# Other PSUM homes, another PE order in the double steps, later rank products and earlier row loads in an SSD and mixture-of-experts kernel

## The chip, the cores and the metric

One NeuronCore of a Trainium2 chip. The metric is the device time of one execution in microseconds (us). A profile of one execution stands beside it. PE is the matrix engine, DVE the vector engine, ACT the scalar engine, POOL is GpSimd, and SP issues the plain transfers. PEld is PE's loading of the standing operand, which runs beside PE's products.

## What is computed

A Mamba2 state-space block over 4 batches, 8 heads, 768 steps, head size 32 and state size 16, and behind it a layer of 8 experts in which each of the 3072 tokens goes to the one expert with the highest logit:

```python
for c in range(nc):                                   # chunks
    cum = np.cumsum(la, axis=-1)
    M = np.einsum('bhin,bhjn->bhij', Cc, Bc) * L      # L: decay between steps, causal
    y_intra = np.einsum('bhij,bhjd->bhid', M, xc)
    y_inter = np.einsum('bhin,bhnd->bhid', Cc, state) * decay_to_i[:, :, :, None]
    y[:, :, sl] = y_intra + y_inter
    state = decay_full[:, :, None, None] * state + np.sum(Bx, axis=2)
...
logits = x @ w_gate                                   # x: (3072, 256), the block's y
expert_idx = np.argmax(logits, axis=1)
for e in range(E):                                    # 8 experts
    h = np.maximum(xe @ w1[e], 0.0)                   # 256 -> 1024
    out[mask] = gate_w[mask, None] * (h @ w2[e])      # 1024 -> 256
```

## The kernel before

The first part works in chunks of 128 steps: 6 chunks x 4 batches make 24 units, two of them make a double step, and a loop runs over 12 double steps d = 0 to 11 (and once more for what is left). Unit n = 2d + s. The work of a double step, with the names that the rows use:

- ACT makes cm (C masked for two heads' halves, `masked_C`), POOL makes xp (x over the running decay, `scaled_x`).
- PE multiplies B and cm into g (`scores`, four PSUM banks), DVE multiplies g with the causal mask into M (`weigh`), PE multiplies M and xp into y (`y_own`) on top of the part from the carried state (`y_old`, lhsT S). y has two banks.
- PE forms the new state in A_ps: B times xp (`own`, eight products of 32x64) and the carried S by an identity product. ACT scales A_ps into S (`state`). A_ps lies in columns 320 to 448 of bank 0 of r.
- ACT copies y to SBUF (`turned`, tile yT). One double step later PE turns it (`rows`, tile r, two banks) so that tokens lie on partitions, which also gives the eight gate logits, and DVE scales r into the token rows and the logits (`rows_out`).

Token rows come in five groups of 6, 6, 4, 2 and 6 units. When a group is complete, `choose` (DVE, one exponential on ACT) finds each token's expert, `rank` (PE) multiplies triangular and all-ones matrices with the choice to count each token's place, DVE picks the place (rb, pos), `gates` and `count` finish, and `place` sends the 128 rows of a unit to x_hbm by an indirect transfer from POOL, two units per double step. After the fourth group `cut` fills up the first 256 rows per expert with zero rows (`lack`), and after the fifth `over` fills the rest.

The second part has 16 jobs: 8 experts with 256 rows each, then 8 with 192 rows each. A job's rows are loaded from x_hbm by SP (`m_load`), transposed in pairs of 128x128 on PE into xT_ps (one bank of its own) and copied by DVE (`m_xT`, `xT_of`), multiplied with w1 into h_ps (three buffers) and through ACT's ReLU into hT (`m_h`), and multiplied with w2 into y_ps one job later (`m_y`, `m_half`), scaled by ACT and sent to the output by POOL. In the middle of a job's h, `between` loads job i+2's rows, transposes job i+1's, and issues the weights of expert i+2. Weights of experts 0 and 1 are loaded inside the first part's loop.

The order is written by hand: each engine does its instructions in the order of the program, and a wait on one holds all behind it. PE, ACT and DVE do not work in one PSUM bank at the same time: where two touch the same bank, the later in the program waits for the earlier. A transfer from x_hbm waits for all earlier placements into it, and a placement for all earlier loads from it. SP issues transfers in order and stops at one whose wait is open.

Of the kernel before, what the change touches and what calls it, by code (L numbers as in the profile page):

```python
# [20 lines left out]
CH = 128  # L21
# [6 lines left out]
CUT = 4  # L28
# [15 lines left out]
def ssd_then_moe(ctx, tc, xs_in, ae_in, wgx, w_gate, w1, w2, gx, gb, gc, ga, out):  # L44
# [63 lines left out]
    A_ps = r_ps[:, 0, 320:448]  # L108

    def early_consts():  # L110
        make_identity(nc, ident)
# [211 lines left out]
    def rank(g):  # L323
# [13 lines left out]
        nc.tensor.matmul(p, lhsT=Tmat, rhs=oh, start=False, stop=True, skip_group_check=True)  # L337
        rb = sm2.tile([128, RG, E], FP32, name="rb")[:, 0:n]
# [63 lines left out]
    def m_load(i):  # L402
        p, e = jobs[i]
        if p == 0:
            xs = mo.tile([128, 2, W], FP32, name="xs", bufs=4)
# [3 lines left out]
        xs = mo.tile([128, 2, W], FP32, name="xs", bufs=4)  # L409
# [9 lines left out]
    def xT_of(xs, pp):  # L419
        p = xT_ps[:, turns[0] % 2]  # L420
# [18 lines left out]
    def up(xT, w, f, n, pp):  # L439
        p = pp.tile([128, 512], FP32, name="h_ps", tag="h", bufs=3)  # L440
# [45 lines left out]
    def general(gp, pp):  # L486
# [4 lines left out]
        with tc.For_i(0, NB) as b, tc.For_i(0, NH) as h:  # L491
# [7 lines left out]
            yp = [pp.tile([128, 512], FP32, name="h_ps", tag="h", bufs=3) for _ in range(2)]  # L499
# [63 lines left out]
    with tc.manual_schedule():  # L563
        load_ae()
# [15 lines left out]
        exs = {}  # L580
        for d in range(ND + 1):
            k = d - 1
            if d < ND:
                y_old(d)
                own(d)
                weigh(2 * d)
                weigh(2 * d + 1)
                if d == 0:
                    decays(1)
                    totals()  # L590
                if d == 1:
                    weakest()
                if d + 1 < ND:
                    for s in range(2):
                        masked_C(2 * d + 2 + s)
                        scaled_x(2 * d + 2 + s, nc.gpsimd)
                y_own(d, 0)
                if d + 1 < ND:
                    scores(2 * d + 2)
            if 0 <= k < ND - 1:  # L600
                rows(k)
            if d < ND:
                y_own(d, 1)
                state(d)
                turned(d)
                if d + 1 < ND:
                    scores(2 * d + 3)
            if 0 <= k < ND - 1:
                rows_out(k)
                u = 2 * k + 1  # L610
                if u == R0[grp[u]] + RGS[grp[u]] - 1:
                    exs[d] = grp[u]
            if d == 0:
                route_consts()
# [3 lines left out]
            if 2 <= d < 10:  # L618
                i = 2 * (d - 2)
                for j in (i, i + 1):  # L620
                    load_w(*divmod(j // 4, 2), j % 4)
            if d in exs:
                q = exs[d]
                e_ = choose(q)
                rank(q)
                gates(q, e_)
                count(q)
                todo += list(range(R0[q], R0[q] + RGS[q]))
                if q == CUT - 1:
                    for n in todo:  # L630
                        place(n)
                    todo = []
                    cut()
                    for i in range(2):
                        m_load(i)
            for _ in range(2):
                if todo:
                    place(todo.pop(0))
        att.close()
# [94 lines left out]
```

## Time and profile before

| what | value |
|---|---|
| median of 3 runs | 354.86 us (354.09 to 356.09) |
| profiled execution | 352.56 us, span 350.8 us |
| PE busy | 289.5 us, 83% of the span |
| DVE, ACT, POOL busy | 70.0, 90.6, 85.6 us |
| mean granted PE clock | 0.918 of full |
| moved by DMA | 36.69 MB, 105 GB/s |

The span runs from the first to the last instruction. The first part fills some 113 us of it, the 16 jobs the rest. PE's busy share is a mean over both parts. A row of the timeline gives the start in us, the time in us, the engine, the line, the operation with its tiles (out<-in), how many instructions are merged, and in brackets the idle time of the engine before it and what ended that.

### The profile page before, as it was taken

The page shows a single profiled execution, that of the slowest core. Times are in us where ns is not written, and L with a number is a line of the kernel's source. Part 1 is how long each engine was busy: PE and PEld are TensorE (multiplying, and loading weights), DVE is VectorE, ACT ScalarE, POOL GpSimd, SP SyncE. Part 2 cuts the span into 40 slices and gives each one's busy share as a digit, 9 for nine tenths or more (in the row PEclk, how much of TensorE's full clock was granted, in tenths as well). Part 3 has the DMA queues.
Part 4 walks back from the last instruction along what each step waited for, and adds up shares of the span by engine and source line. Part 5 has one row for each costly group of instructions (what it writes and reads, how often), then busy time and mean ns, then how long its engine had stood idle before and what let it go on. Part 6 is the DMA issues. An engine that isn't in the chain of part 4 may idle for free.

```text
span 350.8 us, 5397 instructions
## 1 busy us (share of the span) xinstructions
PE 289.5 (83%) x2131; PEld 233.5 (67%) x2131; DVE 70.0 (20%) x168; ACT 90.6 (26%) x265; POOL 85.6 (24%) x171
## 2 busy tenths in 40 slices
PE   2388698596666792599999999999999999999990
PEld 1245465364434571488888888888989889788870
DVE  1736544636335500000000000001000010010000
ACT  2234322323301221013223132232322233223310
POOL 1521182353281187011202112021121111201121
PEclk9999869878668967599999999999999999999998
DMA  7434357450022032795482735100100101100000
GB/s 248 156 132 150 128 201 237 130 187 17 15 103 80 0 107 103 215 341 157 158 252 91 245 104 195 46 32 13 62 30 22 43 23 39 46 2 13 13 34 12
DMA packets 19906, 36.69 MB, mean 105 GB/s; under 512 B 2940, under 2 KB 6751, under 8 KB 19872
## 3 DMA queue, kind: packets, MB, share of 16 engines
q1 hardware_dynamic: 16896, 28.61, 25.4%
q0 software_dynamic: 2976, 7.64, 5.8%
q8 instruction: 19, 0.31, 0.4%
q14 instruction: 15, 0.12, 0.1%
HBM read 28.60 MB, written 8.16 MB: 105 GB/s over the span
## 4 chain that ended last, share of the span: by engine, by line
PE 63%; DVE 12%; issue 10%; POOL 6%; ACT 3%; DMA 2%; another core or an unknown queue 2%; POOLq 0%; SPq 0%; ACTq 0%; DVEq 0%
PE h_ps L443 23%; PE y_ps L473 21%; PE r L280 5%; DVE M L223 4%; PE g L218 4%; PE y L265 4%; POOL x_hbm L349 4%; PE xT_ps L423 3%; PE y_ps L482 2%; ACT S L246 2%; POOL out_dram L457 2%; DVE rows L289 1%; DVE xT L433 1%; DMA xs_n<-in_xs_dram 1%
## 5 line engine op out<-in xcount | busy, mean ns | idle before, releaser
L443 PE MATMUL h_ps<-xT,w 128*128 128x256 f32 (+1 forms) x512 | 106.9, 364 | 0.0
L443 PEld LDWEIGHTS h_ps<-xT,w 128*128 128x128 f32 x512 | 93.1, 197 | 9.0 <-issue 1.2
L473 PE MATMUL y_ps<-w,hT 128*128 128x256 f32 x384 | 85.3, 379 | 0.0
L473 PEld LDWEIGHTS y_ps<-w,hT 128*128 128x128 f32 x384 | 72.7, 190 | 9.5
L452 ACT ACTIVATE hT<-h_ps 128x256 f32<-128x256 f32 (+1 forms) x128 | 45.6, 357 | 84.1 <-PE h_ps L443 76.3
L457 POOL DMA_INDIRECT out_dram<-yo,xs x24 | 23.6, 984 | 167.0 <-ACT yo L463 154.7
L433 DVE COPY xT<-xT_ps 128x256 f32<-128x256 f32 x24 | 10.2, 424 | 182.9 <-PE xT_ps L423 182.9
L463 ACT ACTIVATE yo<-y_ps,xs 128x256 f32<-128x256 f32 x24 | 11.4, 474 | 74.2 <-PE y_ps L473 70.8
L223 DVE TENSOR_TENSOR M<-g,mask 128x1024 f32<-128x1024 f32 x24 | 28.2, 1216 | 4.7 <-PE g L218 4.0
L218 PE MATMUL g<-cm,xs_n 32*128 32x256 f32 x192 | 21.2, 516 | 9.1 <-ACT cm L206 6.2
L349 POOL DMA_INDIRECT x_hbm<-rows,pos x24 | 23.9, 995 | 5.2 <-issue 4.1
L265 PE MATMUL y<-M,xp 128*32 128x128 f32 x384 | 20.3, 338 | 5.4 <-DVE M L223 3.3
L423 PE MATMUL xT_ps<-ident,xs 128*128 128x128 f32 x48 | 10.5, 303 | 15.3 <-DMA xs<-x_hbm 10.6
L280 PE MATMUL r<-turn,yT 128*128 128x160 f32 x96 | 21.3, 379 | 0.0
L280 PEld LDWEIGHTS r<-turn,yT 128*128 128x128 f32 x96 | 17.8, 243 | 5.0 <-issue 5.0
L218 PEld LDWEIGHTS g<-cm,xs_n 32*128 32x128 f32 x192 | 10.0, 229 | 15.8 <-issue 9.0
L211 POOL TENSOR_TENSOR xp<-xs_n,Ei 128x256 f32<-128x256 f32 x22 | 13.7, 636 | 22.9 <-PE y L265 13.3
L246 ACT ACTIVATE S<-r,et 128x32 f32<-128x32 f32 x40 | 8.2, 288 | 42.9 <-PE r L280 35.6
L265 PEld LDWEIGHTS y<-M,xp 128*32 128x32 f32 x384 | 11.5, 130 | 11.4 <-issue 5.8
L423 PEld LDWEIGHTS xT_ps<-ident,xs 128*128 128x128 f32 x48 | 6.1, 148 | 18.7 <-DMA xs<-x_hbm 11.0
L289 DVE TENSOR_TENSOR rows<-r,Er 128x512 f32<-128x512 f32 x12 | 8.3, 692 | 41.2 <-ACT S L246 22.4
L206 ACT ACTIVATE cm<-xs_n,par 128x128 f32<-128x128 f32 x48 | 15.3, 398 | 0.0
(110 smaller groups left out, 128.8 us busy)
## 6 DMA issues: line engine op xcount, KB each, us to landing
w<-in_w_dram SPq DMA_DIRECT2D x64, 256.0 KB
xs_n<-in_xs_dram SPq DMA_DIRECT2D x24, 320.0 KB
xs<-x_hbm SPq DMA_DIRECT2D x8, 258.0 KB
xs<-x_hbm SPq DMA_DIRECT2D x8, 129.0 KB
xh<-x_hbm SPq DMA_DIRECT2D x8, 64.5 KB
x_hbm<-rows,pos POOLq DMA_INDIRECT x24
out_dram<-yo,xs POOLq DMA_INDIRECT x24
turn<-in_wgx_dram SPq DMA_DIRECT2D x1, 160.0 KB
```

Of the source, the lines that this page charges most:

```text
L206: nc.scalar.mul(t[:, u], st[n]["CT"], par[:, u:u + 1])
L218: nc.tensor.matmul(g_ps[:, q, n % 2], lhsT=st[n]["BT"][r], rhs=st[n]["cm"][r].rearrange("p u i -> p (u i)"), start=True, stop=True)
L223: nc.vector.tensor_tensor(out=t, in0=g_ps[:, :, n % 2].rearrange("p q (u i) -> p q u i", u=2), in1=bc(mask[:, None, None, :], [128, 4, 2, ...
L246: nc.scalar.mul(new[:, s, u * D:u * D + D], A_ps[:, 64 * s + u * D:64 * s + u * D + D], et[:, 2 * d + s, u:u + 1])
L265: nc.tensor.matmul(y_ps[o:o + D, h // 4, CH * s:CH * s + CH], lhsT=st[n]["xp"][:, D * h:D * h + D], rhs=st[n]["M"][:, h], start=first, sto ...
L280: nc.tensor.matmul(r_ps[:, s, 160 * t:160 * t + 160], lhsT=sd[d]["yT"][:, t, CH * s:CH * s + CH], rhs=turn[:, t].rearrange("p h e -> p (h ...
L349: s_ = nc.gpsimd.indirect_dma_start(out=x_hbm[:, :], out_offset=bass.IndirectOffsetOnAxis(ap=at, axis=0), in_=row, in_offset=None)
L423: nc.tensor.transpose(p[:, t], xs[:, 128 * t:128 * t + 128], ident)
L443: nc.tensor.matmul(p[:, 0:n], lhsT=w[:, c:c + 128], rhs=xT[:, t, 0:n], start=(t == 0), stop=(t == KT - 1))
L452: nc.scalar.activation(ex[i]["hT"][:, f, 0:n], q, func=ACT.Relu)
L457: return nc.gpsimd.indirect_dma_start(out=out[:, :], out_offset=bass.IndirectOffsetOnAxis(ap=tok, axis=0), in_=yo[:, :], in_offset=None, b ...
L473: nc.tensor.matmul(p, lhsT=ex[i]["hT"][:, f, 128 * t:128 * t + 128], rhs=w_sb[e][1][:, f * DM:f * DM + DM], start=(f == 0), stop=(f == FT ...
```

## The change

Six things change:

- A_ps moves from bank 0 of r to columns 256 to 384 of bank 0 of y. The transposes of the experts' rows move from a bank of their own to the two banks of r, one pair in each in turn; the freed bank is a fourth buffer for h. M has four buffers for three.
- The order inside a double step is another: rows of the step before come first, then own, y_old, both halves of y_own, turned, state, and then both scores of the next step. The loads of the step come at its head, rows_out behind the scores.
- rank, and with it the placing, is done one double step after choose, behind that step's y_own; three placements are issued per double step for two. Group 5's choose and count stand ahead of job 0, its rank in the middle of job 0.
- Of the weights only those of expert 0 are loaded in the loop (double steps 5 to 10); those of expert 1 are issued when the first three jobs' rows have been.
- m_load runs three jobs ahead (three jobs after cut, job 3 at the head of the middle of job 0, then i+3); xs has five buffers for four.
- At the start decays(0) stands ahead of masked_C, one of the first two xp goes to POOL, and a one-element ACT operation stands ahead of all.

```diff
@@
-    A_ps = r_ps[:, 0, 320:448]
+    A_ps = y_ps[:, 0, 256:384]
     def early_consts():
+        nc.scalar.mul(spare, spare, 1.0)
...
-        t = wk.tile([128, 4, 2, CH], FP32, name="M", bufs=3)
+        t = wk.tile([128, 4, 2, CH], FP32, name="M", bufs=4)
...
         nc.tensor.matmul(p, lhsT=Tmat, rhs=oh, start=False, stop=True, skip_group_check=True)
+
+    def ranked(g):
...
         rb = sm2.tile([128, RG, E], FP32, name="rb")[:, 0:n]
...
-            xs = mo.tile([128, 2, W], FP32, name="xs", bufs=4)
+            xs = mo.tile([128, 2, W], FP32, name="xs", bufs=5)
...
     def xT_of(xs, pp):
-        p = xT_ps[:, turns[0] % 2]
+        p = r_ps[:, turns[0] % 2, 0:256].rearrange("p (t m) -> p t m", t=KT)
...
-        p = pp.tile([128, 512], FP32, name="h_ps", tag="h", bufs=3)
+        p = pp.tile([128, 512], FP32, name="h_ps", tag="h", bufs=4)
...
+        nc.vector.memset(spare, 0.0)
         load_ae()
...
         par_consts()
+        decays(0)
         for n in range(2):
             masked_C(n)
             scores(n)
-        decays(0)
         for n in range(2):
-            scaled_x(n, nc.vector)
+            scaled_x(n, (nc.vector, nc.gpsimd)[n])
...
-        for d in range(ND + 1):
+        wq = [5, 6, 7, 8, 9, 9, 10, 10]
+        for d in range(ND):
             k = d - 1
-            if d < ND:
-                y_old(d)
-                own(d)
-                weigh(2 * d)
-                weigh(2 * d + 1)
...
-                y_own(d, 0)
-                if d + 1 < ND:
-                    scores(2 * d + 2)
-            if 0 <= k < ND - 1:
-                rows(k)
-            if d < ND:
-                y_own(d, 1)
-                state(d)
-                turned(d)
-                if d + 1 < ND:
-                    scores(2 * d + 3)
-            if 0 <= k < ND - 1:
-                rows_out(k)
...
+            for j, at in enumerate(wq):
+                if at == d:
+                    load_w(0, *divmod(j, 4))
...
+            if k >= 0:
+                rows(k)
+            own(d)
+            y_old(d)
+            weigh(2 * d)
+            weigh(2 * d + 1)
+            for s in range(2):
+                y_own(d, s)
+            turned(d)
...
+            state(d)
+            q = late.get(d)
+            if q is not None:
+                rank(q)
+                ranked(q)
+                todo += list(range(R0[q], R0[q] + RGS[q]))
+            if d + 1 < ND:
+                for s in range(2):
+                    scores(2 * d + 2 + s)
+            if k >= 0:
+                rows_out(k)
...
                 e_ = choose(q)
-                rank(q)
+                count(q)
                 gates(q, e_)
...
+                late[d + 1] = q
-            for _ in range(2):
+            for _ in range(3):
                 if todo:
                     place(todo.pop(0))
+            if d == ND - 2:
...
+                cut()
+                for i in range(3):
+                    m_load(i)
...
-        xT_ps = pp.tile([128, 2, KT, 128], FP32, name="xT_ps")
         m_xT(0, pp)
         rows(ND - 1)
         rows_out(ND - 1)
+        e_ = choose(CUT)
+        count(CUT)
+        for k in range(8):
+            load_w(1, *divmod(k, 4))
...
                 if i == 0:
+                    m_load(3)
                     q = CUT
-                    e_ = choose(q)
                     rank(q)
+                    ranked(q)
...
-                    if i + 2 < len(jobs):
-                        m_load(i + 2)
+                    if i > 0 and i + 3 < len(jobs):
+                        m_load(i + 3)
                     m_xT(i + 1, pp)
```

PE in a double step of the loop, before. y<-xs_n,S is y_old, r<-xp and r<-S,ident are own with the carried state, y<-M is y_own, r<-turn is rows, g is scores; x4, x8 and x16 count products:

```order
L257 MATMUL y<-xs_n,S 64x128 x8
L232 MATMUL r<-xp,xs_n 32x64 x8
L237 MATMUL r<-S,ident 128x128
L265 MATMUL y<-M,xp 32x128 x8
L218 MATMUL g<-cm,xs_n 128x256 x4
L280 MATMUL r<-turn,yT 128x160 x4
L265 MATMUL y<-M,xp 32x128 x8
L218 MATMUL g<-cm,xs_n 128x256 x4
```

The same engine and step now:

```order
L281 MATMUL r<-turn,yT 128x160 x4
L233 MATMUL y<-xp,xs_n 32x64 x8
L238 MATMUL y<-S,ident 128x128
L258 MATMUL y<-xs_n,S 64x128 x8
L266 MATMUL y<-M,xp 32x128 x16
L219 MATMUL g<-cm,xs_n 128x256 x8
```

The two g stand together at the end, rows at the head, and own and its identity product write into y.

SP from the last weights of the first part to the fourth job's rows, before. xs<-x_hbm are rows of a job, w_1 and w_2 weights of experts 1 and 2:

```order
L164 DMA xs_n<-in_xs_dram 128x640 x2
L176 DMA w_1_88<-in_w_dram 128x512 x4
L406 DMA xs<-x_hbm 128x2x258 x3
L176 DMA w_2_89<-in_w_dram 128x512 x4
L176 DMA w_2_90<-in_w_dram 128x512 x4
L406 DMA xs<-x_hbm 128x2x258
```

Now:

```order
L177 DMA w_0_86<-in_w_dram 128x512 x4
L413 DMA xs<-x_hbm 128x2x258 x3
L177 DMA w_1_87<-in_w_dram 128x512 x4
L177 DMA w_1_88<-in_w_dram 128x512 x4
L413 DMA xs<-x_hbm 128x2x258
L177 DMA w_2_89<-in_w_dram 128x512 x4
L177 DMA w_2_90<-in_w_dram 128x512 x4
L413 DMA xs<-x_hbm 128x2x258
```

In the order before, the third load of the three stands in the program behind group 5's placements; now all of the three and the one behind expert 1's weights stand ahead of them, and the last row here is the first behind them.

DVE behind the rows of a group's last units, before (l to oh_all are choose, rb and pos rank, se and rows<-se gates, cs count, M the next step's):

```order
L299 TENSOR_REDUCE l<-lg_132 128x48
L301 TENSOR_REDUCE mx<-l 128x6
L303 TENSOR_TENSOR sub<-l,mx 128x48
L308 SCALAR_TENSOR_TENSOR eq<-sub,rev_e 128x48
L311 TENSOR_REDUCE m_513<-eq 128x6
L312 TENSOR_TENSOR oh_all<-eq,m_513 128x48
L339 TENSOR_TENSOR rb<-r,oh_all 128x48
L340 TENSOR_REDUCE pos<-rb 128x6
L318 TENSOR_REDUCE se<-ex 128x6
L320 RECIPROCAL rows_127<-se 128x6
L344 TENSOR_REDUCE cs<-oh_all 128x8
L223 TENSOR_TENSOR M<-g,mask 128x1024 x2
```

Now, from the choice's last operation on:

```order
L313 TENSOR_TENSOR oh_all<-eq,m_511 128x48
L351 TENSOR_REDUCE cs<-oh_all 128x8
L319 TENSOR_REDUCE se<-ex 128x6
L321 RECIPROCAL rows_127<-se 128x6
L224 TENSOR_TENSOR M<-g,mask 128x1024 x2
L346 TENSOR_TENSOR rb<-r,oh_all 128x48
L347 TENSOR_REDUCE pos<-rb 128x6
L290 TENSOR_TENSOR rows_128<-r,Er 128x2x256
```

rb and pos, which need PE's rank products, stand behind the next step's M.

## Rows read from the trace of the kernel before

**Rows 1.** The page, part 2: granted PE clock in 40 slices, tenths of full

```profile
PEclk9999869878668967599999999999999999999998
```

**Rows 2.** Busy time by stretch: from:to, length, then busy of each engine, clock, DMA

```profile
26.72:32.86 6.14, 5.30 (x102) 3.51 (x95) 3.15 (x5) 2.46 (x10) 1.23 (x2) 1.00 0.60 194
42.82:51.02 8.20, 8.02 (x78) 5.22 (x75) 3.24 (x5) 1.68 (x7) 7.02 (x16) 0.52 0.61 208
```

**Rows 3.** Timeline of a quiet double step: start, time, engine, operation, [idle before <- ended by]

```profile
29.17 0.71 PE L218 MATMUL g<-cm,xs_n 32*128 32x256 f32 x8 [0.53 <-issue]
29.81 1.35 PE L280 MATMUL r<-turn,yT 128*128 128x160 f32 x8
31.09 0.65 PE L265 MATMUL y<-M,xp 128*32 128x128 f32 x16
31.20 0.82 ACT L246 ACTIVATE S<-r,et 128x32 f32<-128x32 f32 x4 [3.68 <-PE r L280]
31.89 0.60 ACT L270 COPY yT<-y 128x512 f32<-128x512 f32 x1
32.05 0.69 DVE L289 TENSOR_TENSOR rows<-r,Er 128x512 f32<-128x512 f32 x1 [2.99 <-ACT S L246]
32.55 0.67 PE L257 MATMUL y<-xs_n,S 32*64 32x128 f32 x16 [0.17 <-ACT yT L270]
32.86 2.35 DVE L223 TENSOR_TENSOR M<-g,mask 128x1024 f32<-128x1024 f32 x2
33.15 0.43 PE L232 MATMUL r<-xp,xs_n 128*32 128x64 f32 x16
33.51 0.49 PE L237 MATMUL r<-S,ident 128*128 128x128 f32 x2
```

**Rows 4.** Timeline of the double step that completes the first group

```profile
39.12 0.84 DVE L299 TENSOR_REDUCE l<-lg 128x48 f32<-128x384 f32 x1
...
41.30 0.28 PE L335 MATMUL r<-oh_all,ones_bf 128*128 128x40 bf16 x5 [1.83 <-DVE oh_all L312]
...
42.82 2.35 DVE L223 TENSOR_TENSOR M<-g,mask 128x1024 f32<-128x1024 f32 x2
```

**Rows 5.** Timeline from the fourth choice to the last zero rows of the first part

```profile
92.54 0.38 DVE L299 TENSOR_REDUCE l<-lg 128x16 f32<-128x128 f32 x1
...
104.72 0.96 POOL L349 DMA_INDIRECT x_hbm<-zrows,lack  x1 [0.22 <-issue]
```

**Rows 6.** Timeline of jobs 0 and 1: last rank product, placements, row load, transposes

```profile
119.71 0.18 PE L337 MATMUL r<-oh_all,Tmat 128*128 128x48 bf16 x1
...
122.02 1.07 POOL L349 DMA_INDIRECT x_hbm<-rows,pos  x1 [0.56 <-POOL spare L348]
...
123.05 0.69 PE L423 MATMUL xT_ps<-ident,xs 128*128 128x128 f32 x2 [1.09 <-DVE xT L433]
...
138.56 0.96 POOL L349 DMA_INDIRECT x_hbm<-zrows,rest  x1 [0.23 <-issue]
...
141.31 0.36 SPq L406 DMA_DIRECT2D xs<-x_hbm  x1
...
143.93 0.69 PE L423 MATMUL xT_ps<-ident,xs 128*128 128x128 f32 x2 [10.55 <-DMA xs<-x_hbm]
```

**Rows 7.** Timeline of steady jobs: y, h, and the second pair of transposes

```profile
150.20 7.07 PE L473 MATMUL y_ps<-w,hT 128*128 128x256 f32 x32
...
157.10 4.48 PE L443 MATMUL h_ps<-xT,w 128*128 128x256 f32 x20
...
162.32 0.44 PE L423 MATMUL xT_ps<-ident,xs 128*128 128x128 f32 x2 [0.52 <-DVE xT L433]
```

**Rows 8.** Timeline of the start: first g, first M, and the next step's M

```profile
6.23 2.09 PE L218 MATMUL g<-cm,xs_n 32*128 32x256 f32 x16 [6.23 <-ACT cm L206]
...
11.00 2.34 DVE L223 TENSOR_TENSOR M<-g,mask 128x1024 f32<-128x1024 f32 x2
...
20.57 2.36 DVE L223 TENSOR_TENSOR M<-g,mask 128x1024 f32<-128x1024 f32 x2 [3.69 <-PE g L218]
```

More of the change, by code (lines that the diff above doesn't have):

```diff
@@ L337, in rank @@
         nc.tensor.matmul(p, lhsT=Tmat, rhs=oh, start=False, stop=True, skip_group_check=True)
+    def ranked(g):
+        n = RGS[g]
+        sl = slice(R0[g], R0[g] + n)
+        oh = oh_all[:, sl, :]
+        p = r_ps[:, 1, 320:320 + n * E].rearrange("p (n e) -> p n e", e=E)
         rb = sm2.tile([128, RG, E], FP32, name="rb")[:, 0:n]
@@ L498, in general @@
                 nc.sync.dma_start(out=x_t[32 * m:32 * m + 32], in_=gx[ds(r * D, D), :])
-            yp = [pp.tile([128, 512], FP32, name="h_ps", tag="h", bufs=3) for _ in range(2)]
+            yp = [pp.tile([128, 512], FP32, name="h_ps", tag="h", bufs=4) for _ in range(2)]
             for k in range(4):
@@ L574, in ssd_then_moe @@
             scores(n)
[L575 removed]
         for n in range(2):
[L577 removed]
+            scaled_x(n, (nc.vector, nc.gpsimd)[n])
         state_consts()
         todo = []
[L580 to L614 removed]
+        ends, late = {}, {}
+        for g, n in enumerate(RGS):
+            ends[(R0[g] + n) // 2] = g
+        wq = [5, 6, 7, 8, 9, 9, 10, 10]
+        for d in range(ND):
+            k = d - 1
             for n in (2 * d + 6, 2 * d + 7):
@@ L617, in ssd_then_moe @@
                     load(n)
[L618 to L623, printed above, removed]
+            for j, at in enumerate(wq):
[3 more added lines that the diff above has]
+                for s in range(2):
+                    masked_C(2 * d + 2 + s)
+                    scaled_x(2 * d + 2 + s, nc.gpsimd)
+            if k >= 0:
[7 more added lines that the diff above has]
+            turned(d)
+            if d == 0:
+                decays(1)
+                totals()
+            if d == 1:
+                weakest()
+            state(d)
[4 more added lines that the diff above has]
+                todo += list(range(R0[q], R0[q] + RGS[q]))
+            if d + 1 < ND:
+                for s in range(2):
+                    scores(2 * d + 2 + s)
+            if k >= 0:
+                rows_out(k)
+            if d == 0:
+                route_consts()
+            if d in ends:
+                q = ends[d]
                 e_ = choose(q)
-                rank(q)
+                count(q)
                 gates(q, e_)
[L627 to L635, printed above, removed]
-            for _ in range(2):
+                late[d + 1] = q
+            for _ in range(3):
                 if todo:
                     place(todo.pop(0))
+            if d == ND - 2:
+                for n in todo:
+                    place(n)
+                todo = []
+                cut()
+                for i in range(3):
+                    m_load(i)
         att.close()
```

3 lines of the change are left out of this document (1 added, 2 removed).

## Prediction

> **What bounds the kernel now.** I read the page's clock line first, then busy time by stretch, then the timeline of one double step, of one with a choice behind it, and of the change to the experts. The page's span is 350.8 us and the execution took 352.56.
>
> The clock line [rows 1] is full in the expert part (second half) and broken between slices 5 and 18. So two stages have different limits. In the experts PE is dense: a job's 32 products of h and 32 of y take 6.9 us each (y: 7.07 with its tail; h: 4.48 for 20, so 0.216 apiece), some 15 us a job with the transposes [rows 7]. One hole is left there: between the two pairs of transposes PE waits 0.52 us for DVE's copy, because both pairs lie in one bank.
>
> A quiet double step takes 6.14 us, of which PE is busy 5.30 at full clock [rows 2]. The timeline says who is late [rows 3]: rows (29.81) ends at 31.16, ACT's S then runs 0.82 us, DVE's rows waits 2.99 us for S although it reads other columns, and next step's M starts 0.81 us after that. The ring is M, y, g, rows, S, rows on DVE, M. PE's own work is shorter than this ring.
>
> A double step with a choice is worse. l starts at 39.12, PE gets its rank products at 41.30 after 1.83 us of nothing, and the next M starts at 42.82 instead of 3 us sooner [rows 4]: 9.96 us since the M at 32.86. The step behind runs at clock 0.52 and takes 8.20 us [rows 2]. Both together cost 18.2 where two quiet ones cost 12.3: 5.9 us for one choice, and there are four in the loop.
>
> At the change of parts POOL sets the pace. From the fourth choice (92.54) to the end of the last zero rows (104.72 + 0.96) pass 13.1 us [rows 5]. In job 0 PE waits from the last rank product (119.89) to the second pair of transposes (ends 123.74), 3.85 us; then 14 placements run on POOL from 122.02 to 139.52 (1.25 us each), the load of job 2's rows is issued behind them at 141.31, and PE begins at 143.93 after 10.55 us of idling, with slow transposes (0.69 against 0.44) [rows 6].
>
> **The change, part by part.** I build the new span forward from its start; u is the end of the last y in a double step.
>
> *Start.* The table load moves ahead of the data, and the first g goes perhaps 0.3 us earlier, ending near 8.0 [rows 8]. M no longer stands behind two xp on DVE (one goes to POOL): it starts at 8.1 instead of 11.00. From M to the next step's M were 9.57 us; y now follows M directly while decays and totals come behind it, which I take as 8.6 (bounds 7.2 and 9.57). Next M: 16.7 (15.3 to 17.7).
>
> *The double step.* S moves out of the banks of r, so DVE's rows waits for PE alone. What is late next? After u: ACT turns y (0.60) and scales S (0.82), done at u+1.6; PE runs two g until u+1.4 and rows until u+2.75, and only then own, which now shares y's bank and must wait for S. That wait is covered by 1.1 us; with cover gone it would cost its lateness. M starts at u+1.5 and its pair ends at u+3.9; y's two halves come at u+4.3 and u+5.0, so covered too. Hence PE alone: 1.35 + 1.30 + 1.42 + 0.43 + 0.49 + 0.67 = 5.66 [rows 3]; successive starts overlap and give 5.2. I take 5.6, bounds 5.2 and the old 6.14.
>
> *Choices.* DVE's choice starts when rows is done, u+4.9, and keeps DVE some 3.3 us (39.12 to 42.82 less rank's share) [rows 4]. The next M starts at u+8.2 rather than u+7.1, its halves end 9.4 and 10.6, and PE wants them at 9.9 and 10.6. So the choice is hidden; what stays is rank, nine small products, 0.5 us on PE in the step behind (0.3 to 1.0).
>
> POOL now places three rows a step beside two xp: 3 x 1.25 + 1.2 = 5.0 us against 5.6. Tight, but xp is wanted two steps after its place in the queue.
>
> From the M at 16.7 to the M of step 9: 8 x 5.6 + 2 x 0.5 = 45.8, so 62.5 (bounds for the stretch 42.2 and 51.1).
>
> *To the experts.* y of step 9 ends 4.15 later (66.65). In this step rank and rows stand ahead of the fourth choice on DVE, so it starts 2.05 behind, at 68.7. From there POOL still does eight placements, and now a pair of xp stands among them: 13.1 + 1.2, less 0.5 for the rank no longer inside = 13.85, to 82.55. End of placements to load and to PE is 143.93 - 139.52 = 4.4 [rows 6]. Job 0's first transpose: 86.95. PE has no work left by then (two steps of some 7 us behind 66.65 end near 81) and idles about 6 us: the new bound of this stretch. Bounds 22.6 and 28 from step 9's M.
>
> *Jobs 0 and 1.* Transposes and copies 1.9, low clock; rows of the last step 2.6 (1.35 doubled, nearly); h of job 0's first ten pairs 4.48 + 1.4 for low clock; rank 0.5; to the second transposes 3.3 (3.85 less the pair's own 0.52); the rest of h 2.6 + 1.5 for a clock that falls there again, as before; job 1's h 6.9 with 0.9 of transposes; y of job 0 6.9. Sum 33.0, so job 2's h starts at 119.95 where it started at 157.10. The 10.55 us hole is gone because job 2's and 3's rows are loaded ahead of the last placements. Bounds 28.5 (no low clock) and 39 (low to job 1's middle).
>
> What the moved loads touch: weights of expert 1 no longer come in the loop but behind three row loads on SP. At 143.93 eight such pieces were issued within 4 us behind one row load; here they have 15 us until job 1. Job 4's rows wait for all 14 placements (some 17.5 us from about 100) and expert 3's weights stand behind them on SP: issued near 120, wanted near 135. Both hidden; a lateness would stand on PE one for one.
>
> *The rest.* 350.8 - 157.10 = 193.7, less 0.52 for each of the nine later jobs with two pairs, 4.7: 189.0 (188 to 193.7). A fourth h buffer gives nothing: PE does not wait for one [rows 7].
>
> Sum: 119.95 + 189.0 = 309 of span; + 1.76 outside the span = 310.7. The profiled execution lies 2.3 under the median of the runs shown (354.86), so 313. All low ends together make 301, all high ends 333.6; the range leaves a little off both, 303 to 331.
>
> **The rivals.**
> *The clock still falls at each choice* (0.10). Three choices lie before POOL takes over; at 5.9 each [rows 2, 4], 17.7: 331. For it: low stretches follow each choice now. Against: they follow 1.8 us without work on PE [rows 4], and those holes go.
>
> *POOL paces the loop* (0.12). Its 5.0 us, with 0.7 of gates and counts in four steps, is near 5.6, and it stands still while DVE chooses. If a step took 6.5 instead, 8 x 0.9 = 7: 320.
>
> *Slower: PE stays at the low clock through the loop* (0.03). The matmuls of a step take 8.2 at low clock [rows 2], at most 11.2 (twice 5.6); the middle is 9.7, 4.1 more than 5.6. The sum has 42 us to lose, so it decides if all eleven steps stay low: 45 lost, 358. Against: the quiet step pauses 0.84 us in 6.14 and is granted the full clock [rows 1, 2]. The Trainium skill (TensorE: Matmul & The Clock Gate, "A second HAM failure mode: psum-queue depth-cycling") tells of PE pausing briefly between groups of products and swinging between its clocks; by that rule this rival's 358 would hold. The quiet step's row speaks against it.
>
> **How the numbers follow.** Forecast 0.72 (303 to 326, point 313), the clock 0.10, POOL 0.12, slower 0.03, and 0.03 for something outside. The range holds the forecast and POOL and most of the clock's case. About 0.5% is what a measurement of this kernel tells from no change. Faster by more than that 0.95, within it 0.02, slower 0.03.
>
> **What would show it.** Right: from one M pair to the next some 5.6 us in every loop step, with or without choice; clock full from about 20 us until the placements end; DVE's rows waiting for PE and not for S; one hole of some 6 us ahead of job 0's transposes, released by a row load; none ahead of job 2's; 0 in place of 0.52 between transposes. Wrong: own waiting for S or xp, steps of 8 us at clock 0.5, a job waiting for weights, or the row load of job 0 much later than 83.

## The result and the profile after

The changed kernel takes 315.75 us (median of four runs, 314.42 to 317.58), the kernel before 355.23 beside it. The ratio is 0.889, with a 95% interval of 0.884 to 0.895. The profiled execution of after is the 314.42 one, its span 312.6 us. The forecast was 313, with a span of 309.

Busy time by the prediction's five stages, cut at the M of step 1, the M of step 9, the first transpose of job 0 and the h of job 2: first before, then after. Columns are from:to, length, then busy time and count for PE, PEld, DVE, ACT and POOL, granted PE clock, DMA share, GB/s. The kernel before:

```profile
0.00:20.57 20.57, 8.79 (x96) 5.21 (x100) 7.24 (x17) 6.08 (x18) 8.19 (x42) 1.00 0.50 173
20.57:84.61 64.04, 51.13 (x757) 33.82 (x752) 33.57 (x67) 21.65 (x79) 20.83 (x42) 0.87 0.48 160
84.61:112.69 28.08, 18.46 (x192) 12.35 (x191) 12.23 (x31) 3.38 (x11) 13.79 (x29) 0.70 0.20 67
112.69:157.10 44.41, 30.14 (x130) 24.57 (x127) 7.34 (x30) 7.32 (x19) 16.27 (x32) 0.77 0.44 150
157.10:350.80 193.70, 181.00 (x973) 157.59 (x971) 9.59 (x26) 52.20 (x139) 26.55 (x27) 0.99 0.23 74
```

The same view of the changed kernel:

```profile
0.00:15.88 15.88, 8.73 (x87) 5.49 (x87) 6.65 (x17) 7.04 (x22) 8.50 (x43) 1.00 0.62 223
15.88:60.67 44.79, 41.83 (x726) 31.17 (x726) 33.54 (x66) 19.87 (x75) 19.72 (x41) 1.00 0.56 179
60.67:85.29 24.62, 16.06 (x223) 10.83 (x222) 12.76 (x34) 4.35 (x14) 14.81 (x30) 0.86 0.24 81
85.29:119.50 34.21, 29.22 (x127) 24.18 (x128) 7.01 (x28) 6.53 (x18) 15.89 (x32) 0.85 0.61 205
119.50:312.60 193.10, 180.99 (x973) 157.60 (x971) 9.60 (x26) 52.44 (x139) 26.98 (x28) 0.99 0.26 84
```

Of the 38.2 us of span, 37.6 went in the first four stages: 4.7 + 19.3 + 3.5 + 10.2. The last stage, more than half of the kernel, gave 0.6. Against the forecast of each stage:

| stage | forecast us | measured us |
|---|---|---|
| start to the M of step 1 | 16.7 | 15.88 |
| eight double steps | 45.8 | 44.79 |
| M of step 9 to job 0's first transpose | 24.45 | 24.62 |
| to the h of job 2 | 33.0 | 34.21 |
| the rest | 189.0 | 193.10 |

The page's clock line, which answers to [rows 1], is full up to slice 9 (some 70 us) and falls only around the change of parts:

```profile
PEclk9999999995958999999999999999999999999996
```

The timeline of a quiet double step and of the choice behind it, answering to [rows 3, 4]:

```profile
24.79 1.35 PE L281 MATMUL r<-turn,yT 128*128 128x160 f32 x8
24.93 2.36 DVE L224 TENSOR_TENSOR M<-g,mask 128x1024 f32<-128x1024 f32 x2 [1.59 <-PE g L219]
...
26.07 0.43 PE L233 MATMUL y<-xp,xs_n 128*32 128x64 f32 x16
26.44 0.49 PE L238 MATMUL y<-S,ident 128*128 128x128 f32 x2
26.85 0.67 PE L258 MATMUL y<-xs_n,S 32*64 32x128 f32 x16
27.20 0.68 DVE L290 TENSOR_TENSOR rows<-r,Er 128x512 f32<-128x512 f32 x1
27.45 1.08 PE L266 MATMUL y<-M,xp 128*32 128x128 f32 x32
...
28.11 0.85 DVE L300 TENSOR_REDUCE l<-lg 128x48 f32<-128x384 f32 x1
28.46 1.15 PE L219 MATMUL g<-cm,xs_n 32*128 32x256 f32 x16
...
29.54 1.35 PE L281 MATMUL r<-turn,yT 128*128 128x160 f32 x8
...
32.52 0.64 PE L266 MATMUL y<-M,xp 128*32 128x128 f32 x16 [0.25 <-DVE M L224]
33.65 0.64 PE L266 MATMUL y<-M,xp 128*32 128x128 f32 x16 [0.49 <-DVE M L224]
...
35.70 0.28 DVE L292 TENSOR_TENSOR lg<-r,Er 128x128 f32<-128x128 f32 x1
36.12 1.32 PE L281 MATMUL r<-turn,yT 128*128 128x160 f32 x8 [0.35 <-ACT S L247]
```

From one rows to the next (24.79 to 29.54) pass 4.75 us in which PE hardly pauses. DVE's rows stands right behind M with no idle time, where it waited 2.99 us for S before; DVE now waits for PE's g (1.59). So PE sets the quiet step. The choice (from 28.11) makes the next M late: PE waits 0.25 and 0.49 us for M's halves, does rank, and waits 0.35 ahead of the next rows. That row names ACT's S, but rows don't read S. They write r, which DVE's lg must have read first, and lg ends at 35.98, 0.14 us ahead of them; it stands behind rb and pos, which wait for the rank products. When the changed kernel ran again, the same 0.35 behind its second choice was put down to lg.

The change of parts, answering to [rows 5, 6]:

```profile
66.79 0.38 DVE L300 TENSOR_REDUCE l<-lg 128x16 f32<-128x128 f32 x1
...
79.58 0.96 POOL L356 DMA_INDIRECT x_hbm<-zrows,lack  x1 [0.22 <-issue]
...
85.29 0.49 PE L430 MATMUL r<-ident,xs 128*128 128x128 f32 x2 [4.19 <-DMA xs<-x_hbm]
86.30 0.69 PE L430 MATMUL r<-ident,xs 128*128 128x128 f32 x2 [0.52 <-DVE xT L440]
...
97.60 0.44 PE L430 MATMUL r<-ident,xs 128*128 128x128 f32 x2 [1.13 <-DVE f L398]
...
109.24 0.43 DVE L440 COPY xT<-r 128x256 f32<-128x256 f32 x1 [9.78 <-PE r L430]
109.72 0.44 PE L430 MATMUL r<-ident,xs 128*128 128x128 f32 x2 [1.91 <-issue]
```

The hole of 10.55 us ahead of job 2's transposes is gone; a pause of 1.91 us stands near its place. The row puts it down to "issue", that is to nothing that the profile shows; but the second pair starts as DVE's copy of the first ends (109.24 + 0.43), and that copy starts 1.4 us behind the first pair's end (107.81). One hole of 4.19 us is left ahead of job 0. And the 0.52 us between two pairs of transposes is still there, though the pairs now lie in different banks.

### The profile page after: what moved, and what is told of

The parts are those of the page before. It is cut to its first block, busy times and chain, and to the rows that moved or that the text cites. A ratio compares the mean times of both kernels' runs of the same rounds, so it can differ in the third digit from the quotient of the medians.

```text
span 312.6 us, 5387 instructions
## 1 busy us (share of the span) xinstructions
PE 276.8 (89%) x2131; PEld 229.3 (73%) x2131; DVE 69.6 (22%) x168; ACT 90.2 (29%) x266; POOL 85.9 (27%) x172
## 4 chain that ended last, share of the span: by engine, by line
issue 56%; POOL 15%; PE 12%; DVE 8%; DMA 4%; ACT 1%; SPq 1%; POOLq 1%; DVEq 0%; ACTq 0%
POOL out_dram L464 9%; POOL x_hbm L356 5%; DVE M L224 4%; PE r L281 3%; PE y L266 3%; PE g L219 3%; DMA w<-in_w_dram 2%; DMA xs<-x_hbm 1%; DMA x_hbm<-zrows,lack 1%; PE y L258 1%; DVE rows L290 1%; DVE l L300 1%; DMA ae<-in_ae_dram 1%; PE y L233 1%; POOLq L464 1%
## 5 line engine op out<-in xcount | busy, mean ns | idle before, releaser
L450 PE MATMUL h_ps<-xT,w 128*128 128x256 f32 (+1 forms) x512 | 105.0, 360 | 0.0
L440 DVE COPY xT<-r 128x256 f32<-128x256 f32 x24 | 10.2, 425 | 176.4 <-PE r L430 176.4
L266 PE MATMUL y<-M,xp 128*32 128x128 f32 x384 | 17.9, 292 | 6.2 <-DVE M L224 4.2
L281 PE MATMUL r<-turn,yT 128*128 128x160 f32 x96 | 19.1, 350 | 2.1 <-ACT S L247 1.1
L281 PEld LDWEIGHTS r<-turn,yT 128*128 128x128 f32 x96 | 16.0, 221 | 6.2 <-ACT S L247 2.2
L430 PE MATMUL r<-ident,xs 128*128 128x128 f32 x48 | 10.0, 292 | 10.9 <-DMA xs<-x_hbm 4.2
L271 ACT COPY yT<-y 128x512 f32<-128x512 f32 x12 | 7.0, 586 | 43.3 <-PE y L266 30.9
L219 PE MATMUL g<-cm,xs_n 32*128 32x256 f32 x192 | 16.6, 467 | 1.7 <-ACT cm L207 1.7
L430 PEld LDWEIGHTS r<-ident,xs 128*128 128x128 f32 x48 | 6.0, 143 | 14.6 <-issue 7.1
L489 PE MATMUL y_ps<-w,hT 128*64 128x256 f32 x128 | 14.7, 382 | 0.0
L219 PEld LDWEIGHTS g<-cm,xs_n 32*128 32x128 f32 x192 | 10.2, 218 | 3.9 <-ACT cm L207 1.9
```

Of the source, the lines that this page charges most:

```text
L219: nc.tensor.matmul(g_ps[:, q, n % 2], lhsT=st[n]["BT"][r], rhs=st[n]["cm"][r].rearrange("p u i -> p (u i)"), start=True, stop=True)
L266: nc.tensor.matmul(y_ps[o:o + D, h // 4, CH * s:CH * s + CH], lhsT=st[n]["xp"][:, D * h:D * h + D], rhs=st[n]["M"][:, h], start=first, sto ...
L281: nc.tensor.matmul(r_ps[:, s, 160 * t:160 * t + 160], lhsT=sd[d]["yT"][:, t, CH * s:CH * s + CH], rhs=turn[:, t].rearrange("p h e -> p (h ...
L430: nc.tensor.transpose(p[:, t], xs[:, 128 * t:128 * t + 128], ident)
L450: nc.tensor.matmul(p[:, 0:n], lhsT=w[:, c:c + 128], rhs=xT[:, t, 0:n], start=(t == 0), stop=(t == KT - 1))
L489: nc.tensor.matmul(p[64 * u:64 * u + 64, :], lhsT=ex[i + u]["hT"][:, f, 128:P2], rhs=w_sb[e + u][1][:, f * DM:f * DM + DM], start=(f == 0) ...
```

## The experiments

Each group of kernels ran on one chip together with the kernel before. It took 354.55 us beside own tiles, earlier loads, states back in r and rank at once; 354.46 beside the new home alone, the old order, gates later and no placement; 352.02 beside rows two jobs ahead, both additions and two rows a step; and 353.16 beside the changed kernel once more. Across groups, ratios to it are what compares.

### Each pair of transposes in its own tile

```diff
-        p = r_ps[:, turns[0] % 2, 0:256].rearrange("p (t m) -> p t m", t=KT)
-        turns[0] += 1
+        p = pp.tile([128, 512], FP32, name="h_ps", tag="h", bufs=4)[:, 0:256].rearrange("p (t m) -> p t m", t=KT)
```

> The changed kernel, with each pair of transposes in a tile of its own (a turn of the four h tiles) and no longer in the two halves of one tile. Theory: the 0.52 us that PE still waits between the two pairs (for DVE's copy of the first) comes from both halves being one tile, so that the order is kept for the tile and not for the bank. Then the wait is 0 in all 11 places, worth 0.52 x 11 = 5.7 us: 310 against 315.75 for the changed kernel. Rival: the wait is in the work itself (the second pair needs something that DVE writes), or comes back as a wait for ACT to free an h tile, since the transposes now take two of the four turns: 315 to 317.

304.02 us, ratio 0.857 (0.853 to 0.862): 11.7 us under the changed kernel, more than expected. PE's transposes in the rest of the kernel (from the h of job 2), grouped by line, with count, busy us, mean ns, idle us before and what ended it. The changed kernel, whose lines read as those of the kernel before:

```profile
L430 PE MATMUL r<-ident,xs 128*128 128x128 f32 x36 | 7.2, 280 | 2.6 <-DVE xT L440 2.6
L430 PE MATMUL r<-ident,xh 128*128 128x128 f32 x8 | 1.8, 300 | 2.1 <-DVE xT L440 2.1
```

The same groups with own tiles:

```profile
L429 PE MATMUL h_ps<-ident,xs 128*128 128x128 f32 x36 | 6.1, 273 | 0.0
L429 PE MATMUL h_ps<-ident,xh 128*128 128x128 f32 x8 | 1.5, 272 | 0.0
```

The 4.7 us of waits are gone, and no wait for ACT came in their place. So the tile, not the bank, held the second pair back: the program keeps order for a whole tile, and r is one tile of two banks. The rule on banks in the section on the kernel before is to be read so, too. The Trainium skill (PSUM — Partial Sum Buffer, "PSUM bank collisions raise a hardware error") asks for a guard by bank and quadrant; the wait of 0.52 us between different banks goes beyond that.

From job 0's transposes to the h of job 2 pass 25.56 us here and 34.21 in the changed kernel. PE's timeline with own tiles there:

```profile
86.23 1.09 PE L429 MATMUL h_ps<-ident,xs 128*128 128x128 f32 x4 [3.59 <-DMA xs<-x_hbm]
...
89.19 4.48 PE L449 MATMUL h_ps<-xT,w 128*128 128x256 f32 x20
...
94.48 0.63 PE L429 MATMUL h_ps<-ident,xs 128*128 128x128 f32 x4
94.94 7.07 PE L449 MATMUL h_ps<-xT,w 128*128 128x256 f32 x32
```

The transposes at 94.48 no longer wait 1.13 us for DVE to finish reading rank's products, which lay in the same tile (0.52 more behind them). Without these waits the clock comes back sooner: h runs at 4.48 and 7.07 us where it took 5.70 and 8.76. The pause at 109.72 has moved to h of job 2 (two pauses of 1.0 us), so the last stage is only 2.4 us shorter (190.71 against 193.10) and not 4.7. By steps from start to start: 1.6 transposes and rows, 1.2 h, 2.0 rank to h, 1.7 h, 2.1 second transposes, in sum the 8.65.

### Earlier row loads alone, in the kernel before

```diff
-name="xs", bufs=4
+name="xs", bufs=5
...
-                    for i in range(2):
+                    for i in range(3):
                         m_load(i)
...
+                    m_load(3)
...
-                    if i + 2 < len(jobs):
-                        m_load(i + 2)
+                    if i > 0 and i + 3 < len(jobs):
+                        m_load(i + 3)
```

> The kernel before, with one part of the change alone: rows loaded three jobs ahead (job 2's before the last group is placed, job 3's at its head). Theory: the hole of 10.55 us at job 2's transposes goes and nothing else moves: 355.2 - 10.5 = 344.7 (343 to 347). Rival: the hole is replaced by a wait at job 3's rows or at a job's weights, which stand behind the same placements: less than 4 us gained, 351 or more.

Three runs took 345.71 to 346.83 us, which is the expected time, and one 339.41; the kernel before took 354.55. The rival is out, but the size isn't settled: 7.7 to 15.1 us. In the profiled run (346.83) PE waits for no weights and no row load at job 2, and the stage from job 0's transposes to the h of job 2 takes 36.95 us against 44.41. PE's timeline has a pause there:

```profile
138.94 0.69 PE L423 MATMUL xT_ps<-ident,xs 128*128 128x128 f32 x2 [4.01 <-issue]
```

DVE's copy of the first pair starts at 138.46, though the pair ended at 134.93. Whether the run of 339.41 lacked the pause can't be told; it has no profile.

### Rows two jobs ahead, in the changed kernel

The opposite edit: `range(3)` back to `range(2)`, no `m_load(3)`, `m_load(i + 2)`.

> The changed kernel, with one part undone: rows loaded two jobs ahead, so that job 2's stand behind the fourteen placements of job 0 again. Theory: the last placement ends at 115.4, load and landing take 4.4 us more, while job 2's transposes are due at 107.4: PE waits some 12 us, and nothing later gives it back: 326 to 329 against 315.75. Rival: the load is hidden by the faster loop, or the clock's recovery hides it: 316 to 320.

325.66 us, ratio 0.927 (0.923 to 0.930), just under what was expected. The hole is back in PE's timeline, as large as expected:

```profile
117.90 0.69 PE L430 MATMUL r<-ident,xs 128*128 128x128 f32 x2 [12.36 <-DMA xs<-x_hbm]
```

### States back in the bank of r

```diff
-    A_ps = y_ps[:, 0, 256:384]
+    A_ps = r_ps[:, 0, 320:448]
```

> The changed kernel, with one part undone: the states' products stand in the bank of r again. Theory: DVE's rows then wait for ACT's scaled S (0.8 us and its queue) in every step, and since rows, M, y, g is the ring, a step grows from 4.75 by 0.8 to 1.4 us, over nine steps 7 to 13 us: 323 to 329 against 315.75. Rival: the new order of PE (states right behind rows) hides it, since S is done early in the step: within 2 us of 315.75.

339.42 us, ratio 0.960 (0.954 to 0.965), 10 us above the expected range. The wait is the expected one: DVE's rows waits for S, and PE's next rows for DVE. A quiet step takes 6.21 us. What was not expected is what happens at the choices, and that the clock falls behind them. The timeline of a quiet step:

```profile
26.65 0.69 DVE L290 TENSOR_TENSOR rows<-r,Er 128x512 f32<-128x512 f32 x1 [3.06 <-ACT S L247]
...
27.69 0.51 PE L281 MATMUL r<-turn,yT 128*128 128x160 f32 x2 [1.42 <-DVE lg L292]
```

Busy time by stretch (columns as above) of the quiet step ahead of it, of the step with the first choice, of the one behind it, and of the eight steps:

```profile
21.25:27.46 6.21, 4.79 (x90) 3.64 (x90) 3.15 (x5) 2.46 (x11) 1.19 (x2) 1.00 0.30 99
27.46:36.94 9.48, 7.49 (x132) 5.74 (x132) 5.56 (x14) 3.04 (x12) 0.53 (x3) 1.00 0.25 80
36.94:44.34 7.40, 3.90 (x57) 2.48 (x57) 3.52 (x7) 2.46 (x9) 1.91 (x5) 0.78 0.37 126
15.94:82.55 66.61, 48.27 (x760) 36.38 (x760) 33.30 (x65) 20.72 (x76) 19.72 (x41) 0.87 0.36 120
```

The eight steps take 66.6 us in place of 44.8. The quiet step's 1.46 more explain 8 x 1.46 = 11.7 of the 21.8; the rest is in the steps from the first choice on (9.48, 7.40, 10.28 and 10.88 us in a row, where the changed kernel has 6.35, 4.61, 6.08 and 6.93). The clock is only a part of that. The first of them ran at full clock and took 3.27 us more than a quiet step, because DVE's choice (33.79 to 36.94) now stands whole in the ring between rows and M. Behind it PE waits 1.58 and 0.48 us for M's halves and 1.78 for S, since rank writes r too, and the clock of that step is 0.78. In the third, y ended at 49.62, but ACT's copy of it started 2.85 us later, while POOL placed rows:

```profile
52.47 0.59 ACT L271 COPY yT<-y 128x512 f32<-128x512 f32 x1 [9.64 <-remote]
```

The last section comes back to such late starts. So the loss of 24 us holds one of them, and is not the price of the waits for S alone.

### The new home alone, in the kernel before

`A_ps` in y, and `own` ahead of `y_old`.

> The kernel before, with one part of the change alone: the states' products stand in the bank of y and no longer in that of r (and run ahead of the old states' products, so that their first write does not clear those). Theory: the new home alone moves the wait: DVE's rows no longer waits for S, but PE's states now wait for ACT's S and turned copy of y (1.4 us behind the last y, of which two products g cover 0.55), so a quiet double step stays at 6.0 to 6.2 us: 352 to 357. Rival: the home alone takes S out of the ring, PE sets the step with 5.3 to 5.6 us, some 0.6 us in each of eight steps or more: 345 to 350.

351.31 us, ratio 0.992 (0.988 to 0.995): 3 us gained, just under the theory's time and above the rival's. PE waits for ACT's turned y in quiet steps, as the theory says. Its timeline in two steps in a row, of which the first follows a slow start of the loop:

```profile
30.25 0.43 PE L232 MATMUL y<-xp,xs_n 128*32 128x64 f32 x16 [0.57 <-ACT yT L270]
36.29 0.43 PE L232 MATMUL y<-xp,xs_n 128*32 128x64 f32 x16 [0.87 <-ACT yT L270]
```

From one to the other pass 6.04 us. So the wait and the step are the theory's (0.85 and 6.0 to 6.2): the home alone only moves the wait.

### PE's old order, in the changed kernel

```diff
-            for s in range(2):
-                y_own(d, s)
-            turned(d)
+            y_own(d, 0)
+            if d + 1 < ND:
+                scores(2 * d + 2)
+            if k >= 0:
+                rows(k)
+            y_own(d, 1)
...
+            turned(d)
+            if d + 1 < ND:
+                scores(2 * d + 3)
```

With the order, masked_C and scaled_x go back behind the two weigh, and turned behind state, as in the kernel before.

> The changed kernel, with PE's old order in a double step: half of y, half of the scores, rows, the other half of y, the other half of the scores; all else as changed. Theory: the order is what covers ACT's S behind the y of a step; without it PE waits some 0.9 us in each step for S, and the quiet step goes from 4.75 to 6.0 us: nine steps at 1.25, 11 us: 324 to 330, more where the clock falls behind the waits. Rival: the homes in PSUM alone did it: within 3 us of 315.75.

340.83 us, ratio 0.965 (0.959 to 0.971), above the expected range. The quiet step takes 6.03 us, as expected, with a wait of 0.87 for ACT's turned y, which here stands behind S. The rest is in the start (clock 0.77 from 17.91 to 25.23) and in the steps with and behind a choice: 8.86 us at full clock, as the choice adds 2.8 us to the step, and 8.22 at clock 0.79. PE's timeline in the quiet step:

```profile
26.03 0.43 PE L233 MATMUL y<-xp,xs_n 128*32 128x64 f32 x16 [0.87 <-ACT yT L271]
```

So the home alone gives 3 us, and the changed kernel without the home, or without the order, stands at 339 to 341. With both it stands at 316: then PE has no wait left in the quiet step, and the clock holds through three choices. The new order alone in the kernel before was not run.

### Rank at once

```diff
-            q = late.get(d)
-            if q is not None:
-                rank(q)
-                ranked(q)
...
                 e_ = choose(q)
+                rank(q)
+                ranked(q)
                 count(q)
                 gates(q, e_)
-                late[d + 1] = q
+                todo += list(range(R0[q], R0[q] + RGS[q]))
```

> The changed kernel, with one part undone: rank products and their DVE steps stand right behind the choice again, ahead of the gates, and rows are placed from that step on. Theory: PE waits for DVE's choice at each of the four choices (about 1.8 us), the next M starts later by rank's share of some 1 us, and the clock falls behind it: 3 to 6 us for each of three choices in the loop, of which earlier placements give back up to 4 at the end: 322 to 330 against 315.75. Rival: the choice was costly for DVE's sake alone, the place of rank does not matter, and placements that start a step earlier bring the experts forward: 311 to 317.

319.76 us, ratio 0.904 (0.898 to 0.909): slower by 4 us, between the two. The eight steps take 50.6 us in place of 44.8, and 2.6 of that come back ahead of job 0, since rows are placed a step earlier. PE waits 0.56 us for the first choice and not 1.8. Behind it the clock falls in one step only (0.77 from 38.72 to 45.99), where PE waited 2.58 us for ACT's copy of a y that had ended at 35.90. Busy time of the eight steps, columns as above, and that copy:

```profile
15.95:66.51 50.56, 44.67 (x731) 33.64 (x732) 33.61 (x68) 20.22 (x76) 22.88 (x47) 0.97 0.52 166
...
38.91 0.58 ACT L271 COPY yT<-y 128x512 f32<-128x512 f32 x1 [6.77 <-remote]
```

This late start, beside placements, is a part of the 5.8 us; what the place of rank costs without it this run doesn't show.

### Gates later, counts on DVE

`gates` of a group stands behind the next step's two `weigh`, its addition and that of `count` run on DVE, and a step's placements stand ahead of its choice.

> The changed kernel, with the gates of a group worked out behind the next step's M and not ahead of it, the counts and the small addition on DVE and not on GpSimd, and a step's placements ahead of the choice's steps on GpSimd. Theory: DVE's waits inside a choice (0.74 to 0.89 us for ACT's exponential, 0.36 to 0.55 us for GpSimd) are what delays the next M, so the step behind each of three choices in the loop loses 1.5 us less, and the last placements, which now stand 2.7 us behind the fourth choice's gates, start that much earlier: 315.75 - 4.5 - 2.7 = 308.5 (306 to 311). Rival: PE had other work while M was late; only the earlier end of the placements counts: 312 to 314.

314.23 us, ratio 0.887 (0.882 to 0.892): the rival's time, no clear gain over 0.889. The first choice's step falls from 6.35 to 5.78 us, not by 1.5. The third choice's step took 8.56 us (7.16 in the changed kernel): its M started at 62.79, 2.5 us behind the g that it reads (ended 60.27), beside three placements. And job 0's rows came hardly earlier (transposes at 84.96 against 85.29). So this run undervalues the edit; the next but one has it without such pauses.

### No placement within the double steps

```diff
-            for _ in range(3):
-                if todo:
-                    place(todo.pop(0))
```

> The changed kernel, with no row placed within the double steps: all 18 placements of the first four groups stand behind the fourth choice, ahead of the zero rows. Theory: PE's pauses inside its small products, which no semaphore explains (39.62 and 40.36, 44.79 and 45.54, 57.03, 63.72 and 64.46, some 0.3 to 0.6 us each, 2.9 us in all), come from placements that run on GpSimd at the same time. Then they go, and from the M of step 1 to the M of step 9 pass some 41.9 us against 44.8; job 0 comes later, since 18 placements at 1.27 us behind the fourth choice make 12 to 15 us more than now: 327 to 333 in all. Rival: the pauses are PE's own (its code, its queue): they stay, and the stretch keeps its 44.8 us.

328.03 us, ratio 0.927 (0.920 to 0.933). The eight steps take 42.80 us and show no pause that a semaphore doesn't explain. The pauses are now in the y of step 11, beside the 18 placements, where products run by ones and twos (PE's timeline):

```profile
77.26 0.30 PE L266 MATMUL y<-M,xp 128*32 128x128 f32 x2 [0.56 <-issue]
78.69 0.30 PE L266 MATMUL y<-M,xp 128*32 128x128 f32 x2 [1.12 <-issue]
80.10 0.44 PE L266 MATMUL y<-M,xp 128*32 128x128 f32 x2 [1.11 <-issue]
```

So on this chip the pauses go with the placements. Job 0 comes 12 us later, since all placements stand behind the fourth choice.

### Both additions, and two rows a step

Transposes in own tiles with the gates later; and transposes in own tiles with `range(2)` in place of `range(3)` for the placements of a step.

> The changed kernel with both additions at once: transposes in tiles of their own (304.0 by itself) and the gates behind the next M, with counts on DVE and placements ahead of the choice on GpSimd (314.2 by itself, 1.5 us under the changed kernel). Theory: the two touch different stages and add up: 302.5 (301 to 304). Rival: the second only moves GpSimd's placements onto other small products of PE, whose pauses eat what the choice gives back: 304 to 307.

> The kernel with transposes in tiles of their own (304.0), with two rows placed in a double step and not three. Theory: PE's small products pause only where a placement stands beside y; two of three placements of a step fall beside rows and scores, the third beside y, so with two a step the pauses go: from the M of step 1 to that of step 9 pass 43 us against 45.5 in the kernel with three, and the two or three rows that are pushed behind the fourth choice cost 1.3 us each at job 0: 302 to 305. Rival: any placement beside y pauses it and two a step meet y as three do: the stretch stays at 45 us or more, and the end is later: 305 to 309.

295.24 us, ratio 0.838 (0.834 to 0.841), and 299.09, ratio 0.851 (0.847 to 0.855): both below what theory and rival had. Neither shows one of the pauses. But the kernel with rows two jobs ahead, which ran beside them and places three rows a step as the changed kernel does, shows none either. In its timeline the y in which the changed kernel paused twice:

```profile
39.66 1.08 PE L266 MATMUL y<-M,xp 128*32 128x128 f32 x32
```

So two rows a step can't be judged by these runs, and the sum of the two additions is mixed with the missing pauses. Against that kernel the later gates change the three steps with a choice from 6.36, 6.57 and 6.34 us to 5.78, 7.09 and 5.70, and the eight steps by 0.3. The one with later gates is the fastest of all, and beats both kernels: its stretch from the M of step 9 to job 0's transposes is 21.70 us, against 23.18 in the kernel with rows two jobs ahead.

### The changed kernel once more

> The changed kernel once more, nothing edited. Its profile showed PE pausing 0.3 to 0.6 us at a time inside y while rows were placed, 1.9 us once behind the transposes of job 2; the kernel with rows loaded two jobs ahead, whose double steps hold the same instructions, showed none of these pauses, on another chip, and 43.4 us from the M of step 1 to that of step 9 where the changed kernel took 44.8. Theory: the pauses belong to the chip or the moment and not to the program; where they are absent, the stretch takes 43.4 us, job 2's transposes come 1.9 us earlier, and the whole 309 to 312 us. Rival: they belong to this program; they come back at the same products, 44.5 us or more, 314 to 317 in all.

316.42 us, ratio 0.895 (0.892 to 0.898), with the pauses at the same products, 45.44 us for the eight steps, and a larger pause at job 2's transposes. PE's timeline:

```profile
41.12 0.47 PE L266 MATMUL y<-M,xp 128*32 128x128 f32 x8 [0.29 <-issue]
...
111.84 0.44 PE L430 MATMUL r<-ident,xs 128*128 128x128 f32 x2 [2.63 <-issue]
```

The program brings the pauses on this chip too, so the theory falls in its strong form. Kernels on one chip of those used show none with the same double steps (43.41 us). What sets them there or not stays open.

## Why the prediction was right, and which steps failed

**The start.** Right: 16.7 forecast, 15.88 measured, the first M at 7.80 and 8.08 from it to the next. No run takes its parts one by one.

**The ring.** Right. S left DVE's path, M waits for PE, and the quiet step is PE's own work at full clock. The two runs that undo home or order show that either alone leaves a wait of 0.87 to 1.42 us in each step.

**The size of the quiet step.** Too long: 5.6 forecast, bounds 5.2 and 6.14, 4.75 measured. The step took rows' durations of two halves (y 0.65 + 0.65, g 0.71 + 0.71). Started in one run, y follows in 1.01 us and g in 1.08 (27.45 to 28.46 to 29.54). A row's duration reaches past the next row's start (y 0.65 against 0.58 from start to start, g 0.71 against 0.64), and two halves apart take longer than one run even so (1.16 and 1.28 from start to start). Why the seam costs that isn't shown.

**Choices.** Too cheap: "the choice is hidden; what stays is rank". By its sums, with a step of 5.66 us M's halves would have come in time; with 4.75 PE gets there sooner and waits for M and for lg, and a step with a choice takes 6.35 us, 1.6 more than a quiet one. In the kernel without pauses the three cost 1.6, 1.8 and 1.6. The two errors have opposite signs: eight steps were forecast at 45.8 and took 44.79, in part by luck. One row was read loosely: the M at 42.82 came 3.8 us behind its time in a quiet step and not 3; no term rests on it.

**To the experts.** Right: 24.45 forecast, 24.62 measured. The fourth choice's start (66.79 against 68.7) and the last zero rows (80.54 against 82.55) are 2 us early, as the loop is. The hole is 4.2 us and not 6, because PE's last y ended at 81.1, as forecast, while the load came 1.7 us sooner. That PE's time agrees is luck: it left step 9 at 64.9 and not 66.65, and then took 16.2 us and not some 14, as it waited 1.65 and 0.49 us for M behind the fourth choice and the clock fell there.

**Jobs 0 and 1.** Right in sum (33.0 against 34.21), by the low clock it counted with; it did not see that transposes and rank's products now share the tile r, which cost 1.13 us inside the 3.8 that it gave for that place (3.07 measured), nor the pause of 1.91. With own tiles both stretches of h run at full clock (4.48 and 7.07 us), so most of the low clock hung on these waits.

**The moved loads.** Right. The run with rows two jobs ahead brings back a hole of 12.36 us, and no job waits for weights.

**The rest.** The step that failed: "0.52 for each of the nine later jobs, 4.7". The cause given was that both pairs lay in one bank. They lay in one tile, and still do. The stage gave 0.6 us; with own tiles the wait is 0. This one term was missed by 4.1 us, the whole span by 3.6; the other terms nearly cancel. The step from span to median added 1.76 + 2.3 and measured 1.82 + 1.33.

**The rivals.** The clock did not fall at each choice (1.00 through three of them). POOL does not pace the loop (no wait of PE or DVE in it names xp), though its placements go with pauses. The rival with the low clock is no fancy: with S in r, a step with 1.42 us of waits stays at 1.00, but behind a choice, with waits of 1.58, 0.48 and 1.78 us in one step, the clock falls, and the loop stands at 0.87. The Trainium skill (TensorE: Matmul & The Clock Gate, "A second HAM failure mode: psum-queue depth-cycling") describes such swinging; this case shows it there, and with rank at once behind the wait of 2.58 us, but not in quiet steps.

## What to carry to other kernels

Two products in different PSUM banks still wait for each other's readers when both banks are one tile: give what should overlap a tile of its own, and read the wait's releaser before naming its cause. A change of home may be worth little alone and much together with a change of order, when the next wait stands right behind the first and the clock hangs on both. A step that gets faster uncovers what it hid: recompute each cover with the new length, not with the old one.

## What was not expected of the hardware

While POOL issues indirect placements back to back, PE's small products come to a halt with no semaphore to wait for: 0.3 to 0.6 us at a time in y, up to 1.68 us in a row where 18 placements run, and DVE and ACT start late on what PE has finished. At job 2's transposes, beside zero rows, PE waits 1.91, 2.63 and 4.01 us for DVE's copy (the changed kernel, the same once more, earlier loads alone); in the changed kernel ACT's ReLU and DVE's copy both start at 109.2, on products that ended by 107.8. In the loop such starts are 2.5 to 3.0 us late with states in r, rank at once and gates later. Restarts of PE stand some 0.7 us or twice that apart (77.26, 78.69, 80.10). In the three kernels that ran on one other chip nothing of it is seen, though the one with rows two jobs ahead has the same placements in its double steps. The mechanism wasn't found.
